# B step of an interleaved attention kernel: the first piece of O^T gets a PSUM tile of its own, and the deferred output product moves behind the output product in two parts

## The chip, the cores and the metric

The kernel runs on one core of one Trainium2 chip. The metric is the device time of one execution in microseconds (us). The text uses the profile's names for the engines: PE is the matmul engine and PEld its weight loads, DVE the vector engine, ACT the scalar engine, POOL the general engine, and SP the engine that issues most of the DMAs. PSUM is the memory that PE writes its products to, and that DVE and ACT read ("evict") into SBUF.

## The reference

Four layers, A B A B, each applied to the layer norm of the residual x (2048 tokens by 640) and added to it. Layer A is a segment attention with a linear memory; the change doesn't touch it. Layer B goes through 64 segments of 32 tokens in order. Each segment is preceded by 8 memory tokens, and these are the first 8 output rows of the segment before:

```
mem = mem0
for s in range(n_seg):                       # 64 segments
    h = concatenate([mem, x[32 s : 32 s + 32]])      # 40 rows
    q, k, v = h Wq, h Wk, h Wv                       # 32 heads of 128
    scores = where(mask, q k^T * scale, -1e9)        # mask: keys of mem, or key <= query
    o = softmax(scores) v
    o = sum over heads of o Wo                       # 40 rows x 640
    mem = o[:8];  outs.append(o[8:])
```

So step s + 1 cannot start its projections until step s has its first 8 rows. All operands are bf16.

## The kernel before

Layer B is `layer_B` (from line 543). Before its loop it computes K, Q and V of the segment tokens for the first step; after that, each pass of `for s in range(nsteps)` (line 854) does one step with columns `cols_of(u)`, u = s + 1. The 32 columns of a step in `HX` are 8 memory columns, which the step before has to deliver, and 24 token columns. The last 8 tokens of each segment (its tail) don't go through these thin products: their Q, K and V come from `tail_unit` and `vtail_unit`, eight steps' worth at a time, one unit in each step as long as there is another group of eight steps ahead (steps 0 to 54 of a layer). They are stored to DRAM and come back by `tails_load` and `vtails_in`.

The order on PE, ACT, DVE and POOL is written out by hand: `_OrdNC` chains every instruction of these four engines to the one before it in program order, within layer B. SP is not chained; the framework's planner places its DMAs. A wait therefore holds up everything behind it on its engine. Since every instruction goes through that helper, the profile gives nearly all of them line 105; tiles tell them apart.

A step in the order of PE:

1. `thin_mm` for Ka, Qa, Kb, Qb (lines 944 to 951; 20 matmuls each), evicted as `b_kq`: Qa by DVE, the others by ACT.
2. Transposes and scatters into QT and KT, masks, `scores` (lines 953 to 967), then softmax on DVE and ACT (lines 968 to 979), while PE does V (`b_Va`, `b_Vb`) and five of the eight parts of the tail unit (`b_tail`).
3. `p_transp` twice (`b_PTP`), evicted to PTa by ACT and to PTb by DVE; the rest of the tail unit.
4. PV (lines 1002 to 1004): O^T in four PSUM tiles `b_OTP`, one for each row group j of the array, each with room for both halves a of the heads. `pv(0)` writes the half a = 0 of all four, `pv(1)` the half a = 1, 32 matmuls each.
5. Eviction to `OTsb` (lines 1005 to 1008), five casts behind both halves: piece (j 0, a 0) on DVE, tile 1 on ACT, piece (0, 1) on DVE, tile 3 on ACT, tile 2 on DVE.
6. `od_chunk` (line 1011): a quarter of the deferred output product `b_OPSd`, 16 matmuls. It is the output product of the 8 memory rows of four earlier steps, which POOL has put together in `OTdef` (line 1049). The quarters are spread over four steps. When all four are there (steps 7, 11, ..., 63), `od_end` (line 1017) adds the product to `XOd` on DVE and stores it, `tail_dma` loads the next `XOd`, and `od_begin` takes the PSUM tile anew; it has one buffer, so the next product's first matmul waits for the adds. Steps 0 to 3 have no deferred product.
7. The output product `b_OPS` (lines 1012 to 1015): 64 matmuls in eight pairs (j, a), in the order of the eviction.
8. The first four parts of the vtail unit (`b_vtail`); ACT casts the memory rows of `b_OPS` to `b_msb` in two parts; PE brings them into column form (`b_MT`, lines 1034 to 1043), DVE casts these into the next step's `HX`, and the next step's Ka can start.
9. `x_out(ops, XO, ...)` (line 1048): DVE adds the product to `XO` in two instructions, and SP stores it.

After the loop come the four quarters of the last deferred product and its `od_end` (lines 1053 to 1055).

PSUM: the pool `b_ps` has five buffers that are used in turn by everything that calls `ps_tile`; a new tile waits until the one that had its buffer, five allocations earlier, has been read. The pool `b_po` has one buffer each for `b_tail` (and TPbq), `b_OPS` and `b_OPSd`.

Of the kernel before, what the change touches and what calls it, by code (L numbers as in the profile page):

```python
# [18 lines left out]
F32 = mybir.dt.float32  # L19
# [523 lines left out]
def layer_B(nc, tc, C, W, x_src, xb_src, x_dst, mem0, B_Wv, B_Wo, nsteps=64, out_bf16=False, tag=""):  # L543
    SCB = 1.0 / math.sqrt(128.0)
    nc_raw = nc
    nc = _OrdNC(tc, nc_raw, engines=ORDER_ENGINES)
# [4 lines left out]
    with ExitStack() as ctx:  # L551
# [21 lines left out]
        def ps_tile(shape, dtype, name):  # L573
            return pp.tile(shape, dtype, name=name, tag="ps")
# [40 lines left out]
        HX, TX, QT, KT, VH = {}, {}, {}, {}, {}  # L615
        ln_xt, ln_ready = {}, []

        def evac(eng, dst, src, scale=None):
            if eng == "act":
                if scale is None:  # L620
                    nc.scalar.copy(dst, src)
                else:
                    nc.scalar.activation(out=dst, in_=src, func=ACT.Copy, scale=scale)
            else:
                if scale is None:
                    nc.vector.tensor_copy(dst, src)
                else:
                    nc.vector.tensor_scalar(out=dst, in0=src, scalar1=scale, scalar2=None, op0=ALU.mult)
# [29 lines left out]
        def thin_mm(cols_ap, Wt, b, name):  # L658
            ps = ps_tile([128, 512], F32, name)
            for c in range(NCH):  # L660
                for j in range(4):
                    n = 4 * b + j
                    nc.tensor.matmul(ps[32 * j:32 * j + 32, :], lhsT=cols_ap[:, c, :], rhs=Wt[:, c, 512 * n:512 * n + 512],
                                     start=(c == 0), stop=(c == NCH - 1), tile_position=(0, 32 * j), skip_group_check=True)
            return ps
# [50 lines left out]
        def tail_evac(T, k, eng, home=None):  # L716
            proj, hg = divmod(k, 4)
            pool_, tg = home or (wk, "tu")
            tu = pool_.tile([128, 8, 8, 8], BF16, name="b_tu", tag=tg)
            evac(eng, tu[:].rearrange("p s h t -> p h s t"), tail_ps[0][:].rearrange("p h (s t) -> p h s t", t=8),  # L720
                 None if proj else SCB)
            o = 256 * proj + 64 * hg
            nc.sync.dma_start(QKd[8 * T:8 * T + 8, :, o:o + 64].rearrange("s p f -> p s f"), tu[:].rearrange("p s h t -> p s (h t)"))
# [13 lines left out]
        def vtail_evac(T, k, ps, eng, home="vt"):  # L737
            b4, ch = divmod(k, 2)
            vt = wk.tile([128, 256], BF16, name="b_vt", tag=home)
            evac(eng, vt[:], ps[:])  # L740
            for jj in range(2):
                o = 512 * (2 * b4 + jj) + 256 * ch
                nc.sync.dma_start(VTd[8 * T:8 * T + 8, :, o:o + 256].rearrange("s t f -> (s t) f"), vt[64 * jj:64 * jj + 64, :])

        def wo_half(h, jj2):
            return W.wo[:, h, :].rearrange("p (c j x) -> p j c x", j=2, x=64)[:, jj2]

        def d_half(rows, jj2):
            return rows.rearrange("t (c j x) -> t j c x", j=2, x=64)[:, jj2]

        def o_mm(ops_, src_ap_fn, hpairs, first, last):
            for n_, h0 in enumerate(hpairs):
                for e in range(2):
                    for jj2 in range(2):
                        k = 2 * e + jj2
                        nc.tensor.matmul(ops_[32 * k:32 * k + 32, :].rearrange("p (c x) -> p c x", x=64), lhsT=src_ap_fn(h0 + e), rhs=wo_half(h0 + e, jj2),
                                         start=(first and n_ == 0), stop=(last and n_ == len(hpairs) - 1),
                                         tile_position=(0, 32 * k), skip_group_check=True)
# [23 lines left out]
        for nm, b in jobs:  # L782
            ps = thin_mm(cols, W.wk if nm == "K" else W.wq, b, f"b_{nm}p")
# [9 lines left out]
        XO, XOd = init_state()  # L793
# [4 lines left out]
        for b in range(2):  # L798
            ps = thin_mm(cols, W.wv, b, "b_V")
# [7 lines left out]
        def x_out(ops_, XO_, store, nm):  # L807
            nc.vector.tensor_tensor(out=XO_[:], in0=ops_[0:64, :], in1=XO_[:], op=ALU.add)
            if out_bf16:
                xo = wk.tile([64, 320], BF16, name=f"b_xnb{nm}", tag=f"xnb{nm}")  # L810
            else:
                xo = XO_
            nc.vector.tensor_tensor(out=xo[:], in0=ops_[64:128, :], in1=XO_[:], op=ALU.add)
            store(xo)

        def store_head(s):
            def f(xo):
                for jj2 in range(2):
                    nc.sync.dma_start(d_half(x_dst[32 * s:32 * s + 24, :], jj2), xo[32 * jj2:32 * jj2 + 24, :].rearrange("t (c x) -> t c x", x=64))
            return f  # L820

        def tail_dma(s0, store, xo):
            x_ = x_dst if store else x_src
            for jj2 in range(2):
                sb = xo[32 * jj2:32 * jj2 + 32, :].rearrange("t (c x) -> t c x", x=64)
                dr = x_[32 * s0:32 * s0 + 128, :].rearrange("(i t) (c j x) -> i t j c x", t=32, j=2, x=64)[:, 24:32, jj2]
                if store:
                    nc.sync.dma_start(dr, sb)
                else:
                    nc.sync.dma_start(sb, dr)  # L830

        od = {}

        def od_chunk():
            if od:
                k = od["n"]
                OTd = OTdef[(od["s0"] // 4) % 2]
                o_mm(od["ps"], lambda h: OTd[:, h, :], [8 * k + 2 * p_ for p_ in range(4)], k == 0, k == 3)
                od["n"] = k + 1

        def od_end():
            x_out(od["ps"], XOd, lambda xo: tail_dma(od["s0"], True, xo), "d")
            od.clear()

        def od_begin(s0):
            od.update(s0=s0, n=0, ps=po.tile([128, 320], F32, name="b_OPSd", tag="opsd"))
# [4 lines left out]
        def ln_xt_due(s):  # L851
            return s % 8 in (2, 5) and ln_g(s) < NG

        for s in range(nsteps):
# [79 lines left out]
            def pv(a, PTsb, ots):  # L934
                for i in range(4):
                    for part in range(2):
                        for j in range(4):
                            r = slice(32 * j, 32 * j + (8 if part else 32))
                            nc.tensor.matmul(ots[j][:, a, i, :], lhsT=(VH[s] if part else VH[s - 1])[r, a, 128 * i:128 * i + 128],
                                             rhs=PTsb[r, part, i, :], start=(part == 0), stop=(part == 1),  # L940
                                             tile_position=(32 * j, 0), skip_group_check=True)

# [50 lines left out]
            PTa = wk.tile([128, 2, 4, 40], BF16, name="b_PTa", tag="PTa")  # L993
# [3 lines left out]
            PTb = wk.tile([128, 2, 4, 40], BF16, name="b_PTb", tag="PTb")  # L997
            evac("dve", PTb[:], ptpb[:])
            if unit:
                tail_unit(unit[0], unit[1], 5, 8)  # L1000
                tail_evac(unit[0], unit[1], "act")
            ots = [ps_tile([128, 2, 4, 40], F32, "b_OTP") for _ in range(4)]
            pv(0, PTa, ots)
            pv(1, PTb, ots)
            OTsb = wk.tile([128, 32 * 40], BF16, name="b_OTsb", tag="OTsb")
            OTv = OTsb[:].rearrange("p (a x) -> p a x", a=2)
            for j, a0, a1, eng in ((0, 0, 1, "dve"), (1, 0, 2, "act"), (0, 1, 2, "dve"), (3, 0, 2, "act"), (2, 0, 2, "dve")):
                evac(eng, OTv[:, a0:a1, 160 * j:160 * j + 160], ots[j][:, a0:a1, :, :].rearrange("p a i c -> p a (i c)"))
            if not last:
                vtails_in(s + 1)  # L1010
            od_chunk()
            ops = po.tile([128, 320], F32, name="b_OPS", tag="ops")
            order = [(0, 0), (1, 0), (1, 1), (0, 1), (3, 0), (3, 1), (2, 0), (2, 1)]
            for n_, (j, a) in enumerate(order):
                o_mm(ops, lambda h: OTsb[:, 40 * h + 8:40 * h + 40], [16 * a + 4 * j + 2 * ip for ip in range(2)], n_ == 0, n_ == 7)
            if od and od["n"] == 4:
                od_end()
                tail_dma(s - 3, False, XOd)
                od_begin(s - 3)
            elif s == 3:  # L1020
                tail_dma(0, False, XOd)
                od_begin(0)
            if ln_xt_due(s):
                ln_norm(ln_g(s))

# [19 lines left out]
                vtail_unit(unit[0], unit[1], 4, 5, vps)  # L1045
            if unit:
                vtail_evac(unit[0], unit[1], vps, "act")
            x_out(ops, XO, store_head(s), "")
            nc.gpsimd.tensor_copy(OTdef[(s // 4) % 2][:, :, 8 * (s % 4):8 * (s % 4) + 8], OTsb[:].rearrange("p (h c) -> p h c", c=40)[:, :, 0:8])
            if ln_xt_due(s + 1):  # L1050
# [97 lines left out]
```

## Time and profile before

| | |
|---|---|
| median of three runs | 2867.46 us (2866.17 to 2868.26) |
| profiled execution | 2871.54 us |
| its span | 2869.8 us |
| PE busy | 2671.2 us, 93% |
| DVE, ACT, POOL busy | 57%, 54%, 22% |
| mean TensorE clock granted | 0.975 of full |
| B layers in the span | from about 461 to 1465 and from about 1880 to the end, 128 steps |

A line of a group or of the timeline reads: engine, line, operation, out<-in by tile names, partitions by elements and type, count; then busy time and the mean of one instruction (in groups), or start and length (in the timeline). What stands in brackets, or behind the last bar of a group, is the idle time of the engine just before, and what ended it; "issue" means that the engine waited for nothing the profile shows. The chain of waits lists, in order of time, the work that set the end. Matmuls are pipelined and their ends are modelled, so distances between starts say more than lengths.

### The profile page before, as it was taken

The page shows a single profiled execution, that of the slowest core. Times are in us where ns is not written, and L with a number is a line of the kernel's source. Part 1 is how long each engine was busy: PE and PEld are TensorE (multiplying, and loading weights), DVE is VectorE, ACT ScalarE, POOL GpSimd, SP SyncE. Part 2 cuts the span into 40 slices and gives each one's busy share as a digit, 9 for nine tenths or more (in the row PEclk, how much of TensorE's full clock was granted, in tenths as well). Part 3 has the DMA queues.
Part 4 walks back from the last instruction along what each step waited for, and adds up shares of the span by engine and source line. Part 5 has one row for each costly group of instructions (what it writes and reads, how often), then busy time and mean ns, then how long its engine had stood idle before and what let it go on. Part 6 is the DMA issues. An engine that isn't in the chain of part 4 may idle for free.

```text
span 2869.8 us, 145239 instructions
## 1 busy us (share of the span) xinstructions
PE 2671.2 (93%) x64776; PEld 1669.4 (58%) x64776; DVE 1646.2 (57%) x4428; ACT 1555.7 (54%) x3390; POOL 633.2 (22%) x1506
## 2 busy tenths in 40 slices
PE   5899998999999999999969999889999999999988
PEld 2455555666666666665535555556666666666655
DVE  5778854555555555544468878545555555555544
ACT  3777863545445455544438777544455455445533
POOL 3456551100000000000025666400000000010000
PEclk8999999999999999999989999999999999999999
DMA  5110144222221122111130111621111111111110
GB/s 212 53 43 28 33 142 118 44 43 43 44 43 42 42 46 43 40 40 29 23 120 20 57 47 35 198 71 40 42 39 38 43 41 41 42 39 38 38 22 19
DMA packets 322947, 156.40 MB, mean 54 GB/s; under 512 B 245776, under 2 KB 311056, under 8 KB 319248
## 3 DMA queue, kind: packets, MB, share of 16 engines
q1 hardware_dynamic: 320880, 136.63, 18.8%
q8 instruction: 506, 8.29, 1.2%
q10 hardware_dynamic: 1440, 10.49, 1.0%
q14 instruction: 121, 0.99, 0.1%
HBM read 95.65 MB, written 51.38 MB: 51 GB/s over the span
## 4 chain that ended last, share of the span: by engine, by line
PE 61%; DVE 13%; ACT 4%; DMA 3%; issue 2%; POOL 1%; SPq 0%; ACTq 0%; DVEq 0%; POOLq 0%
PE b_OPS L105 11%; PE b_Ka L105 6%; PE b_Qb L105 5%; PE b_Kb L105 5%; PE b_Qa L105 5%; PE b_SP L105 4%; PE b_OTP L105 3%; PE b_OPSd L105 3%; DVE b_ssum L105 3%; PE b_tail L105 2%; PE b_vtail L105 2%; DVE b_negmax L105 2%; PE b_PTP L105 2%; DVE b_SP L105 2%; ACT b_E L105 2%
## 5 line engine op out<-in xcount | busy, mean ns | idle before, releaser
L105 PEld LDWEIGHTS <-b_HX 128*32 128x32 bf16 x15360 | 412.1, 97 | 374.1 <-issue 16.5
L375 DVE TENSOR_REDUCE a_nm<-a_S 128x2 f32<-128x1024 f32 (+3 forms) x512 | 403.5, 811 | 92.3 <-PE a_T L407 70.8
L410 ACT ACTIVATE a_PT<-a_T 128x1024 bf16<-128x1024 f32 (+1 forms) x384 | 341.0, 892 | 51.9 <-PE a_T L407 46.7
L105 POOL COPY b_OTdef<-b_OTsb 128x256 bf16<-128x256 bf16 x128 | 51.2, 400 | 1360.0 <-DVE b_OTsb L105 1288.6
L105 PE MATMUL b_OPS<-b_wo,b_OTsb 128*32 128x320 bf16 x8192 | 327.0, 311 | 12.7 <-issue 7.6
L105 PEld LDWEIGHTS <-b_OTsb 128*32 128x32 bf16 x8192 | 217.0, 100 | 104.2 <-DVE b_OTsb L105 28.1
L412 POOL TENSOR_SCALAR_AFFINE_SELECT a_PT<-a_PT 128x256 bf16<-128x256 bf16 (+1 forms) x384 | 197.3, 516 | 235.6 <-ACT a_PT L410 234.4
L105 ACT CAST b_msb<-b_OPS 128x128 bf16<-128x128 f32 x252 | 61.5, 295 | 294.2 <-PE b_OPS L105 294.2
L105 DVE CAST b_HX<-b_MT 128x16 bf16<-128x16 f32 x248 | 44.2, 178 | 268.8 <-PE b_MT L105 257.5
L105 ACT CAST b_kq<-b_Kb 128x512 bf16<-128x512 f32 x128 | 74.9, 585 | 201.4 <-PE b_Kb L105 201.4
L105 DVE TENSOR_SCALAR b_kq<-b_Qa 128x512 bf16<-128x512 f32 x128 | 88.5, 692 | 157.3 <-PE b_Qa L105 157.2
L105 DVE CAST b_OTsb<-b_OTP 128x160 bf16<-128x160 f32 (+1 forms) x384 | 122.0, 373 | 90.5 <-PE b_OTP L105 90.4
L105 PE MATMUL b_Ka<-b_wk,b_HX 128*32 128x512 bf16 x2520 | 159.2, 381 | 6.0 <-DVE b_HX L105 0.3
L105 PE MATMUL b_Va<-b_wv,b_HX 128*32 128x512 bf16 x2520 | 161.0, 380 | 0.0
L105 PE MATMUL b_Vb<-b_wv,b_HX 128*32 128x512 bf16 x2520 | 160.3, 379 | 0.0
L407 PE MATMUL a_T<-a_q,a_kT 32*128 32x512 bf16 (+3 forms) x1024 | 139.5, 306 | 21.2 <-DVE a_nm L375 14.6
L105 DVE COPY b_KT<-b_TPak 128x128 bf16<-128x128 bf16 x128 | 28.7, 224 | 227.2 <-PE b_TPak L105 227.2
L105 PE MATMUL b_Qb<-b_wq,b_HX 128*32 128x512 bf16 x2520 | 157.9, 379 | 0.0
L105 PE MATMUL b_Qa<-b_wq,b_HX 128*32 128x512 bf16 x2520 | 157.8, 379 | 0.0
L105 PE MATMUL b_Kb<-b_wk,b_HX 128*32 128x512 bf16 x2520 | 157.8, 379 | 0.0
L105 PEld LDWEIGHTS <-b_kq 128*128 128x128 bf16 x2080 | 116.9, 98 | 69.9 <-ACT b_kq L105 55.6
L105 ACT CAST b_kq<-b_Ka 128x512 bf16<-128x512 f32 x128 | 74.9, 585 | 147.0 <-PE b_Ka L105 147.0
(196 smaller groups left out, 5586.7 us busy)
## 6 DMA issues: line engine op xcount, KB each, us to landing
b_QKd<-b_tu SPq DMA_DIRECT2D x128, 128.0 KB
b_tl<-b_QKd SPq DMA_DIRECT2D x128, 128.0 KB
b_wv<-in_B_Wv_dram SPq DMA_DIRECT2D x10, 1024.0 KB
b_wo<-in_B_Wo_dram SPq DMA_DIRECT2D x16, 640.0 KB
b_VTd<-b_vt SPq DMA_DIRECT2D x256, 32.0 KB
b_Vth<-b_VTd SPq DMA_DIRECT2D x512, 16.0 KB
b_XO<-xres SPq DMA_DIRECT2D x256, 30.0 KB
b_wk<-in_B_Wk_dram ACTq DMA_DIRECT2D x5, 1024.0 KB
```

Source lines behind the costliest of these rows:

```text
L105: r = f(*a, **k)
L375: nc.vector.tensor_reduce(out=nm[:, qc, 2 * pr:2 * pr + 2], in_=X[:, :, o:o + w_], axis=AX.X, op=ALU.max, negate=True)
L407: nc.tensor.matmul(Y[:, e, o:o + w_], lhsT=kT[rows, 128 * kc:128 * kc + 128], rhs=q2[rows, 128 * kc:512], start=True, stop=True, tile_posi ...
L410: nc.scalar.activation(out=PT[:, :, b:b + width], in_=Y[:, :, 0:width], func=ACT.Exp, scale=SC)
L412: nc.gpsimd.affine_select(out=dv, in_=dv, pattern=[[0, 2], [0, diag], [1, 128]], compare_op=ALU.is_ge, fill=0.0, base=0, channel_multiplie ...
```

## The change

Piece (j 0, a 0) of O^T gets a PSUM tile of its own (128 x 4 x 40, half as large), and its cast is issued between `pv(0)` and `pv(1)`. Piece (0, 1) gets a fifth tile, allocated after that cast. The order of the other casts becomes tile 1 (ACT), (0, 1) (DVE), tile 3 (ACT), tile 2 (DVE). `od_chunk` can do half of its quarter: its first half (8 matmuls) now follows the first pair of the output product, and its second half follows the whole output product. The pairs of the output product run as (0, 0), (0, 1), (1, 0), (1, 1), then 3 and 2 as before. The block with `od_end`, the load of the next `XOd` and `od_begin` moves from before the vtail unit to just before `x_out(ops, ...)`.

```diff
-        def od_chunk():
+        def od_chunk(part=None):
             if od:
                 k = od["n"]
                 OTd = OTdef[(od["s0"] // 4) % 2]
-                o_mm(od["ps"], lambda h: OTd[:, h, :], [8 * k + 2 * p_ for p_ in range(4)], k == 0, k == 3)
-                od["n"] = k + 1
+                pairs = [8 * k + 2 * p_ for p_ in range(4)]
+                if part is not None:
+                    pairs = pairs[2 * part:2 * part + 2]
+                o_mm(od["ps"], lambda h: OTd[:, h, :], pairs, k == 0 and part != 1, k == 3 and part != 0)
+                if part != 0:
+                    od["n"] = k + 1
...
-                            nc.tensor.matmul(ots[j][:, a, i, :], lhsT=(VH[s] if part else VH[s - 1])[r, a, 128 * i:128 * i + 128],
+                            nc.tensor.matmul(ots[j][a][:, i, :], lhsT=(VH[s] if part else VH[s - 1])[r, a, 128 * i:128 * i + 128],
...
-            ots = [ps_tile([128, 2, 4, 40], F32, "b_OTP") for _ in range(4)]
-            pv(0, PTa, ots)
-            pv(1, PTb, ots)
+            otf = [ps_tile([128, 2, 4, 40] if j else [128, 4, 40], F32, "b_OTP") for j in range(4)]
+            ots = {j: (otf[j][:, 0, :, :], otf[j][:, 1, :, :]) for j in (1, 2, 3)}
+            ots[0] = [otf[0][:], None]
             OTsb = wk.tile([128, 32 * 40], BF16, name="b_OTsb", tag="OTsb")
             OTv = OTsb[:].rearrange("p (a x) -> p a x", a=2)
-            for j, a0, a1, eng in ((0, 0, 1, "dve"), (1, 0, 2, "act"), (0, 1, 2, "dve"), (3, 0, 2, "act"), (2, 0, 2, "dve")):
-                evac(eng, OTv[:, a0:a1, 160 * j:160 * j + 160], ots[j][:, a0:a1, :, :].rearrange("p a i c -> p a (i c)"))
+            pv(0, PTa, ots)
+            evac("dve", OTv[:, 0, 0:160], otf[0][:].rearrange("p i c -> p (i c)"))
+            ot01 = ps_tile([128, 4, 40], F32, "b_OTP1")
+            ots[0][1] = ot01[:]
+            pv(1, PTb, ots)
+            evac("act", OTv[:, :, 160:320], otf[1][:].rearrange("p a i c -> p a (i c)"))
+            evac("dve", OTv[:, 1, 0:160], ot01[:].rearrange("p i c -> p (i c)"))
+            evac("act", OTv[:, :, 480:640], otf[3][:].rearrange("p a i c -> p a (i c)"))
+            evac("dve", OTv[:, :, 320:480], otf[2][:].rearrange("p a i c -> p a (i c)"))
             if not last:
                 vtails_in(s + 1)
-            od_chunk()
             ops = po.tile([128, 320], F32, name="b_OPS", tag="ops")
-            order = [(0, 0), (1, 0), (1, 1), (0, 1), (3, 0), (3, 1), (2, 0), (2, 1)]
+            order = [(0, 0), (0, 1), (1, 0), (1, 1), (3, 0), (3, 1), (2, 0), (2, 1)]
             for n_, (j, a) in enumerate(order):
                 o_mm(ops, lambda h: OTsb[:, 40 * h + 8:40 * h + 40], [16 * a + 4 * j + 2 * ip for ip in range(2)], n_ == 0, n_ == 7)
-            if od and od["n"] == 4:
-                od_end()
-                tail_dma(s - 3, False, XOd)
-                od_begin(s - 3)
-            elif s == 3:
-                tail_dma(0, False, XOd)
-                od_begin(0)
+                if n_ == 0:
+                    od_chunk(0)
+            od_chunk(1)
...
             if unit:
                 vtail_evac(unit[0], unit[1], vps, "act")
+            if od and od["n"] == 4:
+                od_end()
+                tail_dma(s - 3, False, XOd)
+                od_begin(s - 3)
+            elif s == 3:
+                tail_dma(0, False, XOd)
+                od_begin(0)
             x_out(ops, XO, store_head(s), "")
```

## The prediction

> **What bounds the kernel now.** I read the page first: TensorE is busy 93% of the span, and no other engine is above 57%. The chain that ended last is 61% PE.
>
> ```profile
> span 2869.8 us, 145239 instructions
> PE 2671.2 (93%) x64776; PEld 1669.4 (58%) x64776; DVE 1646.2 (57%) x4428; ACT 1555.7 (54%) x3390; POOL 633.2 (22%) x1506
> L105 PE MATMUL b_OPS<-b_wo,b_OTsb 128*32 128x320 bf16 x8192 | 327.0, 311 | 12.7 <-issue 7.6
> ```
>
> So almost any PE pause in a B step is paid in full, and the change can only win a pause that PE has today. I then took the timeline of one undisturbed step (its Ka starts at 1026.65, the next at 1041.62: 14.97 us, a length that recurs through both B layers).
>
> ```profile
> 1037.14 0.40 PE L105 MATMUL b_OTP<-b_PTa,b_Vth 32*128 32x40 bf16 x32
> 1037.38 0.44 PE L105 MATMUL b_OTP<-b_PTb,b_Vth 32*128 32x40 bf16 x32
> 1037.75 0.73 PE L105 MATMUL b_OPSd<-b_wo,b_OTdef 128*32 128x320 bf16 x16
> 1037.95 0.95 DVE L105 CAST b_OTsb<-b_OTP 128x160 bf16<-128x160 f32 x3 [0.67 <-PE b_OTP L105]
> 1038.33 2.36 PE L105 MATMUL b_OPS<-b_wo,b_OTsb 128*32 128x320 bf16 x64
> 1040.51 0.61 PE L105 MATMUL b_vtail<-b_wv,b_TX 128*32 128x256 bf16 x16
> 1040.79 0.49 ACT L105 CAST b_msb<-b_OPS 128x128 bf16<-128x128 f32 x2 [2.07 <-PE b_OPS L105]
> 1041.11 0.21 PE L105 MATMUL b_MT<-b_sel,b_msb 128*32 128x8 bf16 x8
> 1041.39 0.44 DVE L105 CAST b_HX<-b_MT 128x16 bf16<-128x16 f32 x2
> 1041.62 1.05 PE L105 MATMUL b_Ka<-b_wk,b_HX 128*32 128x512 bf16 x16
> ```
>
> Read by starts, since the ends overlap. The deferred product (b_OPSd, 0.58 us to the next group) hides the first eviction: OPS waits for it only about 0.03. Behind OPS, vtail starts at 1040.51 and has 16 matmuls of 0.027 = 0.44, but MT starts 0.60 later: PE waits 0.16 for b_msb. Those are the pauses that the change touches. Third, the chain of waits around a longer step shows a pause with no releaser, between two matmuls of one group:
>
> ```profile
> 594.21 2.21 PE b_OPS L105 x63
> 596.42 0.40 issue
> 596.82 0.29 PE b_OPS L105
> ```
>
> The PE instruction queue brought 8.29 MB in 506 packets, 129,552 PE instructions in all, so 256 to a packet; the longest such pauses (at 564.57, 596.12, 641.20, 717.63 and 749.12) lie whole multiples of 256 PE instructions apart. PE runs out of instructions there, after the fast stretch of transposes and 64 PV matmuls. In the 102 steps that have both a deferred part and a vtail, 30 are stretched between PV and the end of OPS by 0.05 us or more, 15.6 us in all, each step read against the undisturbed one.
>
> **Part 1: first evict early, od split.** The four tiles b_OTP are now awaited through their last PV matmul of the second half, although piece (0,0) is finished with the first. Its own last matmul then comes at 1037.36. From a piece's last PV matmul to the DVE cast it is 0.31 today (1037.64 to 1037.95), so the cast starts at 1037.66, takes 0.32 (128x160 row), and OPS follows 0.06 later (end of cast to first weight load): 1038.04. PE could have gone on at 1037.75, so there is a new pause of 0.29. For the lag the nearest other row is MT to the b_HX cast, 0.23; 0.34 is the most that a PV piece shows. Pause between 0.21 and 0.32; I take 0.29, from the same operation. OPS plus half of od are then 18 groups of four at 0.136 = 2.45, so PE comes out of OPS at 1040.49, against 1040.51.
> The other evictions are needed later than before or as late: (0,1) starts on DVE at 1037.95 and ends 1038.27, wanted at 1038.59 behind od's first half; ACT's two (0.43 each) and DVE's last (0.48) are wanted 0.3 to 0.9 after they end. ACT's queue and SP's loads of the V tails keep their places. The fifth tile takes the slot that the second P^T held, which that half of PV awaits anyway; vtail then takes the slot of piece (0,0), free since 1038.
>
> **Part 2: od's second half behind OPS.** 8 matmuls, 0.27 us. vtail starts at 1040.76, ends at 1041.20; b_msb is ready for 1041.09, so the wait of 0.16 is gone and MT starts 0.09 later than today. From MT to Ka it is 0.51 as before (cast of the first half, then Ka; Ka's later columns need the second cast only 0.2 after it is there). The step is 0.09 longer: 102 x 0.09 = +9.2 us (bounds of the lag: 0.02 to 0.12, +2 to +12).
>
> **Part 3: what the pause gives back.** In a stretched step the missing page of instructions was asked for 256 instructions earlier, before the pause. Every matmul between PV and the end of OPS now comes 0.29 later at the same place in the stream, so min(stretch, 0.29) disappears: summed over the 30 steps, -7.7 us (with a pause of 0.21, -6; nothing at all at worst). The Trainium skill (Runtime: NRT & Kernel Launch, Instruction fetch mechanics) agrees on blocks of 256 instructions but holds that fetching is hidden because the sequencer is slower than the refill; the 0.40 us of "issue" above speaks against it.
>
> **Part 4: steps without od or without vtail.** Steps 0 to 3 of each layer have no od: OPS waited 0.69 after the last PV start and now 0.40, eight times: -2.3. Steps 55 to 62 have no tail work: there PE sits until b_msb in any case, so the second half of od is free and so is the pause (0 to -0.03). But 12 of these 16 take 16.5 to 16.9 us:
>
> ```profile
> 1308.70:1312.10 3.40, 2.26 (x92) 1.00 0.07 15
> 1312.10:1315.50 3.40, 3.40 (x56) 0.51 0.10 25
> ```
>
> (stretches of the windows view: length, PE busy, granted clock.) After 3.4 us with 2.26 busy the clock granted is half for the next 3.4; a window with 2.80 busy kept it. The pause comes 1.7 us behind the softmax wait of 1.2 us, and can join it in one window: 0.25/3.4 of 16 steps, at 1.67 each, +2. In a step at half speed two groups of od (0.24 each) leave the slow stretch for a pause that is there anyway, about 0.15 x 12 = -1.8. Sum 0, from -3 to +7 (all 16 slow).
>
> **Part 5: the deferred x_out and its DMAs, moved behind MT and vtail.** Every fourth step DVE's two adds (0.47 + 0.48) no longer run during OPS but behind the b_HX casts and ahead of XO's two adds. DVE next has b_Qa's eviction, before which it idles 157.3 us in 128 times, 1.23 each: 0.27 is left, so no cost; without that cover it would be 0.97 x 30. On SP its two stores and two loads (0.65 each) go behind vtail's stores and still ahead of XO's; XO's loads come up to 2 us later, land near 596 and are wanted at 598.2 (in the step from 581.84). POOL's copy of O^T stays where it is. At a layer's end there is no cover:
>
> ```profile
> 2858.96 0.47 DVE L105 TENSOR_TENSOR b_XOd<-b_OPSd,b_XOd 64x320 f32<-64x320 f32 x1
> 2861.42 1.34 SPq L830 DMA_DIRECT2D b_XOd<-xres  x2
> 2862.29 2.35 PE L105 MATMUL b_OPSd<-b_wo,b_OTdef 128*32 128x320 bf16 x64
> 2864.95 0.48 DVE L105 TENSOR_TENSOR b_XOd<-b_OPSd,b_XOd 64x320 f32<-64x320 f32 x1 [1.42 <-DMA b_XOd<-xres]
> ```
>
> The last two adds wait for the load of XOd, which stands behind the adds at 2858.96. These now follow od's second half, behind OPS: about 2862.29 + 0.27, less the 0.2 by which OPS may end earlier, + 0.3 to the cast = 2862.6. The whole chain of adds, stores and loads moves by 3.6 (2.5 if this step ran at full clock). PE's last 64 matmuls also have to wait for these adds now (one PSUM tile), but end near 2866.1, ahead of the load at 2868.5. In the first B layer the same chain runs from the adds at 1441.92 over XOd's load to the a_xt load that lands at 1461.1, and PE idles 9.50 before the next transposes; OPS ends there at 1443.7, so adds 1.0 to 2.4 later: +1.7.
>
> **Sum.** 9.2 - 7.7 - 2.3 + 0 + 3.6 + 1.7 = +4.5 us on the profiled execution, 2871.54 (span 2869.8 and 1.7 around it): 2876.0. The median of the three runs is 2867.46, 4.1 less, so 2872.0, +0.16%. What a measurement here can tell from no change is 0.2%, 5.7 us: 2861.7 to 2873.2.
>
> **Rivals.** *The pages come no earlier (0.14).* The pause then saves no stretch: +12.2, 2879.7. For it: two such packets start at different distances from the pause they cause, 1.0 to 1.5 before it. The skill's rule, fetching never binds, would give the same +12.2.
> *The cast starts sooner (0.18).* With 0.23 of lag, pause 0.21: 102 x 0.02 - 6 - 2.9 + 5.3 = -1.6, 2866. For it: one piece alone is awaited, not four; against: the lag of its own operation.
> *Faster (0.08).* The cast starts as soon as the modelled 0.17 of its own matmul is over. Pause 0.16: steps -0.04 x 102 = -4, pages -4.6, steps without od -3.4, ends +5.3 = -6.7, 2860.8. It decides from a lag under 0.18; no row shows one.
> *Clock (0.10).* The pause tips all 16 short steps and a few more windows into half clock: 4.5 + 7 or more, 2879 to 2885. Against it: in steps with tail work a window is mostly above 2.8 busy of 3.4. The skill (TensorE: Matmul & The Clock Gate, Why this matters for your kernels) warns of idle gaps above about 3 us; here 1.2 us in one window is enough.
> *The early cast isn't early (0.05).* If it still waits for the second half, the pause is 0.58: 102 x 0.38 - 12 + 3 = +30, 2897.
>
> **How the numbers follow.** The forecast has 0.45, at 2872.0, its own range 2868 to 2877; 4 in 10 of it lie above 2873.2. Slower: 0.19 + 0.14 + 0.10 + 0.05 = 0.48. Faster: 0.08 and a little of the early cast, 0.11. The rest, 0.41, is within 0.2%. Range 2862 to 2883: a tenth below (faster), a tenth above (a late cast, the worst of the clock).
>
> **What would show it.** In an undisturbed step: OPS 0.66 after the second half of PV starts (0.95 now), one DVE cast of b_OTsb beginning before the last PV matmul is 0.1 old, od in two rows of 8, no wait of MT for b_msb, Ka to Ka 15.06. Fewer pauses marked "issue" within OPS. At the end, b_XOd's load issued near 2865 and the last adds near 2868.5. The forecast is wrong if the undisturbed step is under 15.00 or over 15.10, if stretches within OPS stay at 15 us, or if more than 13 short steps are slow.

## The result and the profile after

| | before | changed |
|---|---|---|
| median of 12 executions each, us | 2867.40 (2862.50 to 2883.96) | 2877.38 (2873.70 to 2892.39) |
| ratio, 95% interval | | 1.0033 [1.0017, 1.0049] |
| second timing (20 and 8 executions), us | 2861.93 | 2874.82 |
| ratio, 95% interval | | 1.0032 [1.0017, 1.0047] |
| profiled execution / its span, us | 2871.54 / 2869.8 | 2874.62 / 2872.9 |

The ratios are those of the paired comparison, not quotients of the medians. The change makes the kernel 0.3% slower. The page of the changed kernel, its span, engines and the group of the output product (columns as in the fences above):

```profile
span 2872.9 us, 145220 instructions
PE 2657.9 (93%) x64776; PEld 1692.4 (59%) x64776; DVE 1649.4 (57%) x4428; ACT 1556.9 (54%) x3390; POOL 636.1 (22%) x1506
L105 PE MATMUL b_OPS<-b_wo,b_OTsb 128*32 128x320 bf16 x8192 | 344.6, 311 | 30.5 <-DVE b_OTsb L105 28.3
```

PE has the same share of busy time as before, but what it idles for ahead of the output product has changed. Before, most of 12.7 us was "issue" (7.6). Now 28.3 of 30.5 us is the wait for DVE's cast. The view of the tile b_OPS says how often:

```profile
its engine sat idle before it (us, times) until:
...
  DVE b_OTsb L105: 28.3, 127
  issue: 1.5, 5
```

That is 0.22 us in nearly every step, and the waits without a releaser are down to 1.5. The timeline of one undisturbed step (its Ka starts at 1239.29, the next at 1254.39, 15.10 us; as in the timelines further on, rows that do not bear on the point are left out):

```profile
1249.78 0.40 PE L105 MATMUL b_OTP<-b_PTa,b_Vth 32*128 32x40 bf16 x32
1250.02 0.47 PE L105 MATMUL b_OTP<-b_PTb,b_Vth 32*128 32x40 bf16 x32
1250.33 0.95 DVE L105 CAST b_OTsb<-b_OTP 128x160 bf16<-128x160 f32 x3 [0.39 <-PE b_OTP L105]
1250.70 0.46 PE L105 MATMUL b_OPS<-b_wo,b_OTsb 128*32 128x320 bf16 x8 [0.22 <-DVE b_OTsb L105]
1250.98 0.45 PE L105 MATMUL b_OPSd<-b_wo,b_OTdef 128*32 128x320 bf16 x8
1251.26 2.08 PE L105 MATMUL b_OPS<-b_wo,b_OTsb 128*32 128x320 bf16 x56
1253.16 0.45 PE L105 MATMUL b_OPSd<-b_wo,b_OTdef 128*32 128x320 bf16 x8
1253.43 0.61 PE L105 MATMUL b_vtail<-b_wv,b_TX 128*32 128x256 bf16 x16
1253.44 0.49 ACT L105 CAST b_msb<-b_OPS 128x128 bf16<-128x128 f32 x2 [2.05 <-PE b_OPS L105]
1253.87 0.20 PE L105 MATMUL b_MT<-b_sel,b_msb 128*32 128x8 bf16 x8
1254.39 0.62 PE L105 MATMUL b_Ka<-b_wk,b_HX 128*32 128x512 bf16 x8
```

OPS starts 0.68 after the second half of PV (0.95 before), its first and second group are parted by half of od, the other half of od runs at 1253.16, and MT follows vtail by 0.44 (0.60 before), without a wait for b_msb. The output product does not end sooner than before (its last matmul starts 3.26 us after the first of PV in the median of the 102 steps, before 3.25), and 0.27 us of od now stand between it and MT.

### The profile page after: what moved, and what is told of

Its sections match the earlier page's. It is cut to its first block, busy times and chain, and to the rows that moved or that the text cites. A ratio compares the mean times of both kernels' runs of the same rounds, so it can differ in the third digit from the quotient of the medians.

```text
span 2872.9 us, 145220 instructions
## 1 busy us (share of the span) xinstructions
PE 2657.9 (93%) x64776; PEld 1692.4 (59%) x64776; DVE 1649.4 (57%) x4428; ACT 1556.9 (54%) x3390; POOL 636.1 (22%) x1506
## 4 chain that ended last, share of the span: by engine, by line
PE 60%; DVE 14%; ACT 5%; issue 3%; DMA 2%; POOL 1%; SPq 0%; DVEq 0%; ACTq 0%; POOLq 0%
PE b_OPS L105 11%; PE b_Ka L105 6%; PE b_Kb L105 5%; PE b_Qa L105 5%; PE b_Qb L105 5%; PE b_SP L105 4%; DVE b_ssum L105 3%; PE b_tail L105 2%; PE b_OPSd L105 2%; PE b_vtail L105 2%; DVE b_negmax L105 2%; PE b_OTP L105 2%; PE b_PTP L105 2%; DVE b_SP L105 2%; ACT b_E L105 2%
## 5 line engine op out<-in xcount | busy, mean ns | idle before, releaser
L105 PE MATMUL b_OPS<-b_wo,b_OTsb 128*32 128x320 bf16 x8192 | 344.6, 311 | 30.5 <-DVE b_OTsb L105 28.3
```

Of the source, the lines that this page charges most:

```text
L105: r = f(*a, **k)
```

## The experiments

The tables use sums that I worked out from the traces, step by step: the undisturbed step (the shortest, from Ka to Ka, of the 102 steps that have both od and vtail); the stretches (what these 102 steps take from the start of the last PV matmul to that of the last OPS matmul beyond their median, with the number of steps that are 0.05 us or more beyond it); and the end, from the last step's Ka to the end of the span.

### The kernels before and after, profiled again

`look_before` and `look_after` are the two kernels unchanged.

> The kernel before, unchanged, for a second profile. If the stretches within OPS (15.4 us over 30 of 102 steps) and the 11 slow ones of the 16 short steps belong to the kernel, they come out alike, within 3 us and 2 steps. If they belong to the execution, they differ, and the difference of the two profiled spans, 3.1 us, says less than the timed runs.

> The changed kernel, unchanged, for a second profile. Same question: stretches 5.6 us over 17 steps, 10 slow short steps, undisturbed step 15.10, end 26.7. The undisturbed step and the end should be the same to 0.02; the stretches and the slow steps alike only if they belong to the kernel.

| us | before, twice | changed, twice |
|---|---|---|
| span | 2869.8, 2866.5 | 2872.9, 2869.3 |
| undisturbed step | 14.964, 14.965 | 15.099, 15.096 |
| stretches (steps) | 15.4 (30), 14.5 (30) | 5.6 (17), 5.6 (15) |
| steps 0 to 3 of both layers | 120.7, 121.0 | 119.5, 118.6 |
| steps 55 to 62, both layers | 258.6, 256.4 | 257.0, 256.7 |
| of these 16 longer than 16 us | 11, 10 | 10, 10 |
| end | 23.0, 23.3 | 26.7, 26.9 |

What the change does to a step, to the stretches and to the end repeats, and the stretches and the slow steps of one kernel come out alike, within the 3 us and 2 steps that were expected. Nor does the time that leaves the stretches turn up elsewhere in the steps: outside the stretches, the 102 steps take 13.5 and 14.3 us beyond the undisturbed step before, and 13.6 and 11.2 in the changed kernel. Two executions of one kernel still differ by 3.3 to 3.6 us in span. So the differences by place are used below, and a difference of two spans is not.

### One part alone: the early cast, or the split

`e2_early_only` keeps piece (0, 0) in its own tile with its early cast, and puts od back whole ahead of OPS, with `od_end` in its old place:

```diff
+            od_chunk()
             ops = po.tile([128, 320], F32, name="b_OPS", tag="ops")
...
-                if n_ == 0:
-                    od_chunk(0)
-            od_chunk(1)
+            if od and od["n"] == 4:
+                od_end()
...
```

> Early eviction alone: the first piece in its own tile, cast between the PV halves; the deferred product undivided between PV and the output product, its x_out in its old place. Theory (the pause ahead of OPS is what took the stretches within OPS away): no pause longer than 0.03, undisturbed step 14.95 to 14.99, and the stretches between PV and the end of OPS come back to about 15 us over some 30 of 102 steps (5.6 us over 17 in the changed kernel). Steps 0 to 3 gain 0.29 each. Time: kernel before, less about 2 us. Rival (the stretches fell because of the new tiles or the other order of casts): they stay near 6 us and the time is about 10 us less than before. The second half of PV, 0.28 in the changed kernel and 0.26 before, stays 0.28 if the cast beside it lengthens it.

`e3_split_only` does the reverse: od in two parts behind OPS's first pair and behind OPS, `od_end` moved, but all five casts behind both PV halves and from the old tiles:

```diff
+            ots = [ps_tile([128, 2, 4, 40], F32, "b_OTP") for _ in range(4)]
             pv(0, PTa, ots)
-            evac("dve", OTv[:, 0, 0:160], otf[0][:].rearrange("p i c -> p (i c)"))
-            ot01 = ps_tile([128, 4, 40], F32, "b_OTP1")
...
             pv(1, PTb, ots)
```

> The split and the move alone: eviction as before behind both PV halves, the deferred product's first half behind the first pair of OPS, its second half behind OPS, x_out moved. Theory: the pause ahead of OPS is 0.58 (OPS 0.69 after the last PV start); the undisturbed step is 14.97 + 0.38 = 15.35; of the stretches only what exceeds 0.58 in each step is left, 3 us in place of 15; steps 0 to 3 as before; the end 3.7 later. 39 - 12 + 4 = about 30 us more than before. Rival (the stretches don't depend on the pause): they stay between 6 and 15 us, and the time is 34 to 43 us more than before. The second half of PV is 0.26 again.

| us | median (executions) | ratio, 95% interval | undisturbed step | stretches (steps) |
|---|---|---|---|---|
| e2_early_only | 2862.26 (12) | 0.9996 [0.9983, 1.0009] | 14.949 | 12.1 (26) |
| e3_split_only | 2909.56 (5) | 1.0165 [1.0147, 1.0182] | 15.360 | 2.1 (9) |

The timeline of an undisturbed step of e3_split_only:

```profile
2012.35 0.44 PE L105 MATMUL b_OTP<-b_PTb,b_Vth 32*128 32x40 bf16 x32
2012.92 0.95 DVE L105 CAST b_OTsb<-b_OTP 128x160 bf16<-128x160 f32 x3 [0.66 <-PE b_OTP L105]
2013.30 0.46 PE L105 MATMUL b_OPS<-b_wo,b_OTsb 128*32 128x320 bf16 x8 [0.51 <-DVE b_OTsb L105]
```

The cast starts 0.57 after the second half of PV starts (0.31 in the changed kernel) and nothing is left in front of OPS to hide it, so PE idles 0.51 in each step. With od whole in front, on the other hand, the early cast alone wins only what OPS waited before:

```profile
849.17 0.95 DVE L105 CAST b_OTsb<-b_OTP 128x160 bf16<-128x160 f32 x3 [0.40 <-PE b_OTP L105]
849.26 0.73 PE L105 MATMUL b_OPSd<-b_wo,b_OTdef 128*32 128x320 bf16 x16
849.82 2.35 PE L105 MATMUL b_OPS<-b_wo,b_OTsb 128*32 128x320 bf16 x64
```

In e2_early_only the first of the three casts, 0.32 long, is done by 849.49. OPS could follow 0.05 later, as it does in the changed kernel, but od keeps PE until 849.82, so about half of od's 0.56 hides nothing any more. The stretches are at 12.1 us, much nearer to the 15 of before than to the 6 of the changed kernel, so neither the new tiles nor the other order of the casts took them away.

In e3_split_only the step and the stretches came out as expected (15.360 for 15.35, 2.1 us for 3), and its traces add up to 31 us more than before, as was worked out. The timing missed: 46 to 47 us, more than even the rival's 34 to 43. The section on the clock comes back to that.

### Half of od ahead of the output product

So `e4_half_ahead` is the changed kernel with od's first half moved from behind OPS's first pair to ahead of OPS:

```diff
+            od_chunk(0)
             ops = po.tile([128, 320], F32, name="b_OPS", tag="ops")
...
-                if n_ == 0:
-                    od_chunk(0)
             od_chunk(1)
```

> The changed kernel with one move: the deferred product's first half (8 matmuls, 0.27 us) stands ahead of the output product, between PV and the first pair, where it covers the first eviction. Theory: no pause ahead of OPS (under 0.03), OPS ends 0.27 earlier, the second half behind OPS still covers the wait for b_msb: undisturbed step 14.82 (14.97 before, 15.10 changed); stretches come back to about 15 us; 102 x -0.15 = -15, steps 0 to 3 -2, end +4: about 13 us less than before, 23 less than the changed kernel. Rival (PE is bound by the rate at which its instructions come): the stretches grow by what the steps gain, to 25 us or more, and the time is within 5 us of before.

Measured: 2846.31 (6 executions), ratio 0.9942 [0.9927, 0.9957]; undisturbed step 14.824, stretches 11.8 (23 steps), end 26.75. That is 17 us less than before, by the ratio, where 13 were expected. The timeline:

```profile
907.74 0.47 PE L105 MATMUL b_OTP<-b_PTb,b_Vth 32*128 32x40 bf16 x32
908.05 0.95 DVE L105 CAST b_OTsb<-b_OTP 128x160 bf16<-128x160 f32 x3 [0.40 <-PE b_OTP L105]
908.14 0.46 PE L105 MATMUL b_OPSd<-b_wo,b_OTdef 128*32 128x320 bf16 x8
908.43 2.36 PE L105 MATMUL b_OPS<-b_wo,b_OTsb 128*32 128x320 bf16 x64
```

PE's work is the same as in the changed kernel and in the same tiles, and only eight matmuls stand elsewhere. OPS starts at nearly the same distance from PV (0.69), but half of od is already done by then. The step is 0.275 shorter than that of the changed kernel, which is that pause: the other distances (PV, last OPS matmul to MT, MT to Ka) are the same to 0.003.

### The last step as before

`e1_last_step` is the changed kernel, and `e5_half_ahead_last` is e4_half_ahead, each with od whole and `od_end` in its old place in the last step of each layer:

```diff
+            if last:
+                od_chunk()
...
-            od_chunk(1)
+            if not last:
+                od_chunk(1)
+            else:
+                od_end()
+                tail_dma(s - 3, False, XOd)
+                od_begin(s - 3)
```

> The changed kernel, but in the last step of each B layer the deferred product is undivided ahead of the output product and its x_out stands behind the output product, as before the change. Theory (the chain adds, stores, load of XOd, last adds sets the end): the stretch from the last step's first Ka matmul to the end of the span falls from 26.7 us (changed kernel) to about 23.0 (kernel before: 22.99), so about 3.6 us less than the changed kernel, all other steps alike (undisturbed step 15.10). Rival (PE's last 64 matmuls or the last stores set the end): it stays at 26 to 27.

> The last experiment's kernel (first half of the deferred product ahead of the output product), and in the last step of each B layer the deferred product undivided ahead of the output product, its x_out right behind it. Theory: the end from the last step's first Ka falls from 26.8 to about 23.1, undisturbed step 14.82 as there; 3.6 us less than there, about 20 less than before in time. Rival: the end stays, no difference.

| us | median (executions) | ratio, 95% interval | end | undisturbed step |
|---|---|---|---|---|
| changed, as in the first timing | 2877.38 (12) | 1.0033 [1.0017, 1.0049] | 26.7 | 15.10 |
| e1_last_step | 2872.00 (6) | 1.0034 [1.0020, 1.0049] | 23.3 | 15.09 |
| e4_half_ahead | 2846.31 (6) | 0.9942 [0.9927, 0.9957] | 26.8 | 14.82 |
| e5_half_ahead_last | 2846.14 (8) | 0.9942 [0.9923, 0.9961] | 22.8 | 14.82 |

The traces show the end 3.4 to 4.0 us shorter. In the changed kernel its timeline is

```profile
2861.60 0.44 PE L105 MATMUL b_OPSd<-b_wo,b_OTdef 128*32 128x320 bf16 x8
2862.10 0.48 DVE L105 TENSOR_TENSOR b_XOd<-b_OPSd,b_XOd 64x320 f32<-64x320 f32 x1 [3.94 <-PE b_OPSd L105]
2864.60 1.34 SPq L830 DMA_DIRECT2D b_XOd<-xres  x2
2868.05 0.48 DVE L105 TENSOR_TENSOR b_XOd<-b_OPSd,b_XOd 64x320 f32<-64x320 f32 x1 [3.90 <-DMA b_XOd<-xres]
```

and in e1_last_step, where the span ends at nearly the same time but the last step began 3.3 later,

```profile
2860.62 1.26 PE L105 MATMUL b_OPSd<-b_wo,b_OTdef 128*32 128x320 bf16 x16
2861.66 3.50 PE L105 MATMUL b_OPS<-b_wo,b_OTsb 128*32 128x320 bf16 x64
2861.93 0.48 DVE L105 TENSOR_TENSOR b_XOd<-b_OPSd,b_XOd 64x320 f32<-64x320 f32 x1 [0.45 <-PE b_OPSd L105]
```

The adds that complete this deferred product wait for od's second half, behind all of OPS, in the one kernel, and only for od ahead of OPS in the other. The intervals of the ratios, 0.3 to 0.4% wide, do not resolve these 4 us; below, at equal clock, one of the two pairs points that way and the other does not.

### V tails behind the memory rows

`e6_vtail_behind` goes one step further from e5_half_ahead_last. Before MT only three parts of the vtail unit are left, and the other two fill MT's own waits:

```diff
-                vps = vtail_unit(unit[0], unit[1], 0, 4)
+                vps = vtail_unit(unit[0], unit[1], 0, 3)
...
-                    if unit and pi == 0:
-                        vtail_unit(unit[0], unit[1], 4, 5, vps)
+                    if unit:
+                        vtail_unit(unit[0], unit[1], 3 + pi, 4 + pi, vps)
```

> As the kernel with the half ahead and the old last step, and the fourth and fifth parts of the vtail unit moved one place back: the fourth between the two parts of MT, the fifth behind the second part, where PE waits 0.30 for the b_HX cast. Theory: MT then starts when b_msb is ready, 0.73 after the last OPS start (0.835 there), and the vtail part fills the wait: undisturbed step 14.71 to 14.73; 102 x 0.11 = 11 us less than the half ahead with the old last step, about 31 less than before. Rival (b_msb's second part or the casts then hold MT up): step 14.80 or more, no gain.

Measured: 2835.22 (4 executions, 2832.13 to 2838.85), ratio 0.9896 [0.9877, 0.9915]; undisturbed step 14.712, stretches 11.3 (25 steps). The timeline:

```profile
911.93 0.50 PE L105 MATMUL b_vtail<-b_wv,b_TX 128*32 128x256 bf16 x12
911.93 0.49 ACT L105 CAST b_msb<-b_OPS 128x128 bf16<-128x128 f32 x2 [1.78 <-PE b_OPS L105]
912.25 0.21 PE L105 MATMUL b_MT<-b_sel,b_msb 128*32 128x8 bf16 x8
912.32 0.28 PE L105 MATMUL b_vtail<-b_wv,b_TX 128*32 128x256 bf16 x4
912.48 0.24 PE L105 MATMUL b_MT<-b_sel,b_msb 128*32 128x8 bf16 x12
912.57 0.28 PE L105 MATMUL b_vtail<-b_wv,b_TX 128*32 128x256 bf16 x4
912.78 0.83 PE L105 MATMUL b_Ka<-b_wk,b_HX 128*32 128x512 bf16 x12
```

MT starts 0.32 behind vtail instead of 0.44, 0.725 after the last OPS matmul (0.835 in e5_half_ahead_last), and the last part of vtail runs where PE waited for b_HX. So the step is 0.108 shorter, 11 us in 102 steps, as expected. This is the fastest kernel here, 1.0% ahead of the kernel before.

### The short steps, and the clock

`e7_short_as_before` is the changed kernel, with od whole and ahead of OPS in the steps without tail work; `after_again` is the changed kernel, timed beside it.

```diff
+            if not unit:
+                od_chunk()
             ops = po.tile([128, 320], F32, name="b_OPS", tag="ops")
...
-                if n_ == 0:
+                if n_ == 0 and unit:
                     od_chunk(0)
-            od_chunk(1)
+            if unit:
+                od_chunk(1)
```

> The changed kernel, but in the steps without tail work (55 to 63 of each layer) the deferred quarter stays undivided ahead of the output product, so these steps have no pause of 0.29 us in front of it. What is to be told apart is why the timings give +9.4 us where the two profiled executions of each kernel give +3. Theory A (clock): the pause makes some more of the short steps fall to half clock. The mean granted clock over the 12 timed runs of the changed kernel is 0.9730, against 0.9751 and 0.9740 in two sets of the kernel before, and within the kernels timed so far a thousandth of clock goes with 2.0 us. Then this kernel has a mean clock about 0.0015 above the changed kernel and saves 3 us by it; with 3.4 us for the end of the last step (its adds no longer stand behind a second half of the deferred quarter), it is 6 to 7 us under the changed kernel. Theory B (pages): the clock is the same, the timed executions only gain less from the stretched steps. Then the mean clock is that of the changed kernel within 0.0007 and the time is 3 to 4 us under it, all from the end. Under both the undisturbed step is 15.10 and the stretches are about 5 us.

> The changed kernel once more, on the chip and beside the runs of the kernel before that the run above has. Theory A (clock): mean granted clock lower than that of the kernel before by 0.001 to 0.002, and 2 to 4 of the difference of 9 us go with it. Theory B (pages): mean clocks within 0.0007, the difference of 8 to 11 us stays at equal clock. If the difference itself is 3 to 5 us here, the 9.4 of the first timing was partly the chip.

Measured: e7_short_as_before 2868.83 (12 executions), ratio 1.0023 [1.0005, 1.0041], mean granted clock 0.9732; after_again 2874.82 (8), mean clock 0.9735; the kernel before beside them 2861.93 (20), 0.9746. Undisturbed step 15.09 in both, end 23.0 and 25.3. The mean clock of e7_short_as_before is that of the changed kernel, where theory A asks for 0.0015 more; the difference of two such means is uncertain by 0.001, so theory A is unsupported rather than excluded. Its time is 6.0 lower, as theory A said; the end explains 2.3 to 3.9 of that, by the three profiles of the changed kernel, and the rest is open.

Most of the scatter of the executions does go with the clock. Over the 123 timed executions of all kernels, with a level of its own for each kernel and set, 0.001 of mean clock goes with 1.99 us (standard error 0.12). Read at a clock of 0.974, with the account that the traces give beside it (102 undisturbed steps, the stretches, steps 0 to 3 and the end, against the mean of the two profiles of before; for the changed kernel the mean of three):

| at clock 0.974, against before (2865.2, 50 executions) | timed, us | by the traces, us | of it stretches |
|---|---|---|---|
| changed (20 executions) | +9.8 | +5.9 | -8.9 |
| e1_last_step | +4.8 | +0.2 | -11.2 |
| e7_short_as_before | +3.2 | -0.3 | -11.0 |
| e2_early_only | -3.5 | -7.1 | -2.9 |
| e3_split_only | +38.3 | +31.4 | -12.9 |
| e4_half_ahead | -18.2 | -15.5 | -3.2 |
| e5_half_ahead_last | -18.8 | -24.2 | -7.1 |
| e6_vtail_behind | -29.8 | -30.7 | -3.7 |

(The standard error of a level is 0.4 to 1.3.) The order agrees, and so do the large sizes; e3_split_only's 46 us become 38, since its mean clock is 0.9714. The first row mixes two timings. The 12 executions of the first stand at 2876.3, but the kernel before that was timed beside them (2867.40, higher than in any other set) has no clocks on record and is not among the 50. The 8 of the second stand at 2873.0, 7.5 above the 20 of before beside them, and that is the sounder figure. Against these 8, e1_last_step and e7_short_as_before are 3.0 and 4.6 lower, about what the end asks for. e4 and e5 show no such step. In six of the eight rows the timed value lies 3.5 to 7 above the account. Two readings were not told apart: part of what the traces credit to the stretches may be missing in the other executions (for e2_early_only that is not enough, 3.6 above with 2.9 credited), or the two profiles of before may simply be long ones: the first, 2871.54 at clock 0.975, lies 8 us above the timed executions of that clock, the second 1.

## Why the prediction was right or wrong

The forecast was 2872.0, +4.5 us; measured was +9 by the ratios. The range held it, and the sign was right; the forecast itself lay on the inner side of the 0.2% bound and the result outside it. The terms that the traces show add up to +5.6 (the +5.9 of the table and -0.3 for the transition). That this is near +4.5 is in part luck: the step cost 4.2 more than forecast, while the pages gave 1.2 more and the transition cost 2.0 less. Of what the timings show beyond +5.6, about 2 goes with the clock and the rest is open.

**The pause (Part 1) was right.** OPS starts 0.408 after the last PV matmul, by starts, where 0.40 was said (the profile counts only 0.22 of the pause as idle time, since the modelled ends of the last PV matmuls reach into it). The rival that the cast starts sooner falls by this: at its lag of 0.23, OPS would start at 0.32. The rival that the early cast isn't early falls too; e3_split_only shows what that would have been: 0.695, a step of 15.36.

**Behind OPS (Part 2) was right.** From the last OPS matmul to the first of MT it is 0.834, before 0.724: +0.11, as 0.27 less 0.16 gives.

**The undisturbed step was mis-sized: +0.13 instead of +0.09.** The two pieces that were costed at nothing are missing. The second half of PV takes 0.276 from first to last start where it took 0.256, together 0.520 instead of 0.500 for all of PV. It is 0.520 in every kernel with the early cast (e1, e2, e4 to e7) and 0.500 in e3_split_only. The extra 0.02 lies wholly ahead of the last four PV matmuls, which start 0.054 behind the four before them instead of 0.033; the early cast is recorded as starting 0.03 after that. Whether the cast, its wait or the smaller tiles cause it was not separated. And from MT to Ka it is 0.522 instead of 0.505 ("0.51 as before"): 0.522 also in e3 and e4, 0.505 in e2, where MT still waits for b_msb; why it grows is not shown. 102 x 0.135 = +13.8 instead of +9.2 (0.131 and +13.4 by the means of all profiles). This is the term of the sum that failed most. The bound of 15.10, above which the prediction called itself wrong, was kept by 0.001 to 0.008.

**The pages (Part 3): mechanism right, size open.** Predicted -7.7 of 15.6. In three profiles of the changed kernel 5.6, 5.6 and 7.0 are left of 15.

That the pauses wait for instructions can be read from the packets of PE's instruction queue, 506 of 16 KB in each trace. In the two profiles of before there are 45 places where two OPS matmuls start more than 0.3 us apart. At each of them PE goes on 1.25 to 1.66 us after an instruction packet has landed, whether the pause was 0.3 or 1.3 us long; in the blocks without such a pause the median from the landing to the instruction at the same place is 3.0 to 3.2 us, and about a tenth lie under 1.7. What the prediction says of the asking, 256 instructions earlier, no record shows: these packets start 81 to 225 PE instructions ahead. Nor are the five pauses that it lists the longest: the longest in that trace is 1.32 us, at 2577.36.

The dose was varied: with a pause of 0.03 or none ahead of OPS (before, e2, e4, e6) 11 to 15 us of stretches, with 0.29 (changed, e1, e7) 4 to 7, with 0.58 (e3) 2.1. e5 is the exception, with 7.9 without a pause, so one execution can be off by some 4 us. The rival that the pages come no earlier falls for the profiled executions; for the timed ones part of the gain may be missing. The Trainium skill (Runtime: NRT & Kernel Launch, Instruction fetch mechanics) has fetching mostly hidden. In this kernel it is hidden at most of the 506 blocks, but not within OPS, where 15 us are lost to it and a pause of PE gives most of them back.

**Steps 0 to 3 (Part 4): right.** -2.3 predicted; -1.2 and -2.4 in the two pairs of profiles, -1.9 in the third profile against the mean of before.

**Short steps: 0 predicted, and nothing seen in the traces** (-1.6 and +0.3 in the two pairs, +2.1 in the third profile). The rival of the clock has not come true there: 10, 10 and 12 slow steps of 16, against 11 and 10. The mean clock of the 20 timed executions is 0.9732 against 0.9746 for 50 of before. By the slope that is 2.8 us (2.2 in the second timing alone), not counted in the sum; where it comes from is open.

**The end (Part 5): +3.6 predicted, +3.7 and +3.6 measured** in the first two pairs, +2.2 in the third profile. In that one the last step runs at full clock, for which 2.5 was said; in the other two a half-clock stretch of 3.4 us falls on its output product. The chain went as described: adds at 2862.10, load issued at 2864.60, last adds at 2868.05.

**The transition after layer 1: +1.7 predicted, -0.6 and 0.0 measured** (from the last step's Ka to the first Ka of the next B layer, 450 us later). Measured from the last step's Ka, in the first pair, the adds are 3.8 later, more than the 1.0 to 2.4 that was said. But the delay shrinks on its way: XOd's load is issued 2.4 later, the second adds run 1.0 later, the a_xt load is issued 1.0 later and its data are used 0.4 later. In the second pair the adds are 3.9 later and the load 1.8, but the second adds run 0.7 sooner; the two profiles of before differ by 2.2 there themselves. The step that failed is carrying the whole delay along a chain of DMAs as if no link of it had slack; where the slack lies was not tested.

## What to carry to other kernels

Work that hides an eviction may only be moved away as far as the eviction itself has been moved: half of od was enough to cover the cast that comes 0.26 sooner, and none was too little, at 0.275 us a step (0.9942 against 1.0033 by the ratios). Moving filler work behind a product pays only where the engine waits there, so two moves that belong together are best costed one at a time. An edit in a loop has a price at the loop's last pass as well, where a chain of adds, stores and loads is hidden by nothing.

## What the runs showed of the hardware

- From the start of the last PV matmul into the first tile of O^T to DVE's first cast out of it, it is 0.340 us before and 0.329 in the changed kernel, where 32 matmuls into other tiles follow and the last of them starts only 0.03 before the cast. So the cast waits for its own tile alone.
- The pauses within OPS come with the instruction blocks of 256. With the PE instructions and weight loads numbered in order, all 45 pairs of OPS matmuls that start more than 0.3 us apart in the two profiles of before lie on one or two pairs of neighbouring remainders modulo 256, and 21 of 22 in the first two profiles of the changed kernel. PE goes on 1.25 to 1.66 us after the packet of the block has landed, and a pause of 0.29 in front of OPS halves their number.
- The half-clock stretches, 3.41 us long, are not a property of the kernel alone: 6 to 13 of the 16 short steps are slow in the profiles of these kernels, at 1.5 to 1.8 us each. The Trainium skill (TensorE: Matmul & The Clock Gate, What's actually happening) says that the activity window runs freely, so that the point at which the clock changes depends on where in the window the first matmul lands. The traces agree that the same work is hit or missed: one such stretch falls on the last output product in two profiles of the changed kernel, and none in the third.
